# Attention with an exponential on two engines: two of VectorE's four shifted forms summed by an accumulating transfer, with six shared homes

## The chip, the cores and the metric

The kernel runs on one core of a Trainium2 chip. The metric is the device time of one execution in microseconds (us). Before the change it is 793.76 us, the median of three runs (793.5 to 793.86). The core's engines that matter here are TensorE (PE, matrix products), ScalarE (ACT, exponentials and tanh), VectorE (DVE, elementwise work), GpSimd (POOL) and the queues that issue transfers (SP's above all). They run side by side, each through its own instructions in program order, and wait for each other by semaphores.

## The reference

Two blocks read the same x (2048 rows of 512, bfloat16) and are mixed row by row by a gate:

```python
qkv = (x @ wqkv) in 32 heads of 16            # x: 2048 x 512, wqkv: 512 x 1536
p = softmax(q @ k.T * 16 ** -0.5)             # per head, 2048 x 2048
a = (p @ v) @ wo                              # attention
b = (silu(x @ w_gate) * (x @ w_up)) @ w_down  # 512 -> 1792 -> 512
g = sigmoid((x * gate_w).sum(-1))
out = g * a + (1 - g) * b
```

The costly part is the softmax: 32 heads x 2048 x 2048 exponentials, some 134 million.

## The kernel before

**Units and tiles.** Queries are cut into 4 blocks of 512 (`QB`), heads into 8 groups of 4 (`G`); a block and a group make one of 32 units. A unit has 16 tiles of 128 keys (`KT`); a tile is 4 heads x 128 keys x 512 queries. The scores of a tile come as two pairs of heads; the product with the values adds up in one PSUM bank for the whole unit (`o_ps`), which VectorE copies out at the unit's end (`post`, called from `close`). The values have a column of ones beside each head's 16, so that the softmax's denominator comes out of the same product.

**Two ways to the exponential.** For most tiles ACT takes it from a pair's scores, 128 x 1024 at a time (`emit_pair`, tiles `s_t` to `e_t`), and PE multiplies the result with the values in one group of four column matmuls (`pv`). For the others PE writes the scores of one head after another into `d_t`, often beside a pair's score matmuls in rows of the array that those leave free, and VectorE computes (`emit_d`, `first`) a 16-bit integer `y_t` = EXP_A x score + EXP_B, whose bits, read as bfloat16, are a coarse power of two. It then makes four copies of the whole tile, (y + shift) x 0.25 with four shifts (`copy`, tiles `c_t`), and PE multiplies each of the four with the values: the sum of the four forms is the smoother exponential. Such a tile thus costs VectorE four times 128 x 512 from PSUM and four times 128 x 2048 in SBUF, and PE four groups of column matmuls where a tile of ACT's costs one.

**Homes.** A copy lies in one of `NS` = 4 homes, taken in turn: three buffers of the pool `vex`, and one that is the first head group's keys (`kaug[:, 0]`) once these are used up, or four rows of `wd_t` before. The profile therefore shows copies under three names, `c_t`, `kaug` and `wd_t`. A home comes free when the product of its copy has run. ACT's results have `EB` = 10 buffers.

**The order of the work.** The order of every engine's instructions is written out when the program is built, by a planner (`Plan`) that keeps a clock for each engine: 0.216 us for a group of column matmuls and for a pair of scores, 0.1 for a change between row and column use of the array, 0.906 for an exponential (`ACT_US`), 0.6 for a VectorE instruction. In the main loop it emits the next pair of scores when the bank it needs comes free, and fills PE's time before that with products (`emit_pv`) and with pieces of other work (`side`, `put_piece`): projections, the feed-forward block's `gu` and `ops` chains, gate logits. These pieces wait in chains with a release and a due slot (`Pacer`). `fill_dve` gives VectorE its work by the plan's clock. `v_unit` says whether a further tile may go to VectorE: its work must end 8 us (`LEAD`) before the unit's exponentials do. `want_d` says how many `d_t` may be emitted now, from the three spare PSUM banks (`banks`), less one if a column chain is next. `hi[un]` is the number of ACT's tiles in a unit. If `EB - 1` pairs wait for their product, a product is forced (`next_pv`).

**The gate.** `gate_pieces` multiplies x with `gate_w` in eight visits of eight matmuls with one column each (`glog`), and clips each result on VectorE into `ge`; `gate_end` takes the exponential. `gate_w` is loaded by `late_loads`, called at slot 28 in program order; SP's queue runs ahead of that, as nothing there waits. The values of heads 4 to 31 come from `v_pieces`, 16 chains of four groups (`vp`, 448 columns each).

All matmuls go through one helper line (L160), all ACT instructions through L163, VectorE's and SP's through L172, so groups are told apart by tile names.

Of the kernel before, what the change touches and what calls it, by code (L numbers as in the profile page):

```python
# [9 lines left out]
ALU = mybir.AluOpType  # L10
AX = mybir.AxisListType
BF16 = mybir.dt.bfloat16
F32 = mybir.dt.float32
U16 = mybir.dt.uint16
# [65 lines left out]
def kernel(  # L80
# [32 lines left out]
    SLOTS = UNITS * KT  # L113

    UNIT = [(qb, 0) for qb in range(QB)] + [(qb, g) for qb in range(QB) for g in range(1, G)]
    EB = 10
    NY = 3
    NV = 4
    NC = 4
    NS = 4  # L120

# [49 lines left out]

    vec = Ordered(nc.vector)
    queue = Ordered(nc.sync)


    xT = big.tile([P, DC, S], BF16, name="xT")
# [24 lines left out]
    wo_l = big.tile([P, 2, D], BF16, name="wo_l")  # L203

    def late_loads():
        queue.dma_start(out=gw_col[:], in_=gate_w.rearrange("(dc p) -> p dc", p=P))
        queue.dma_start(out=wo_t[:], in_=A_wo.rearrange("(b p) d -> p b d", p=P))
        for i in range(2):
            for j in range(4):
                h = H - 8 + 4 * i + j  # L210
                queue.dma_start(out=wo_l[32 * j + 1:32 * j + 1 + DH, i, :], in_=A_wo[h * DH:(h + 1) * DH, :])
# [92 lines left out]
    def spend(mode, mms, ready=0.0):  # L304

        plan.seq += 1
        work_at.append((plan.pe, mms))
        plan.pe = max(plan.pe + (0.1 if mode != plan.mode else 0.0), ready) + (0.226 if mode == "F" else 0.216) * mms
        plan.mode = mode

    def later(cost, f, ready=None, key=None):

        c = plan.chain
        if c is not None:
            c.owed += 1
        ready = plan.pe + 0.25 if ready is None else ready
        owed.insert(sum(o[0] <= ready for o in owed), (ready, cost, f, c, key))
# [41 lines left out]
    def m_free(ps, t):  # L359
        i = [h is ps for h in held].index(True)  # L360
        banks[i], held[i] = t + 0.2, None
# [137 lines left out]
    def v_pieces(tt):  # L499

        def end(p):
            dst = vaug[:, tt, 4 * VC:G * 4 * VC].rearrange("p (h c) -> p h c", c=VC)[:, :, 1:1 + DH]
            vec.tensor_copy(out=dst, in_=p[:, 64:D].rearrange("p (h c) -> p h c", c=DH))
            m_free(p, plan.dve)
        return columns(DC, "vp", lambda dc: xT[:, dc, tt * P:(tt + 1) * P], lambda dc: wv[:, dc, 64:D],
                       lambda p: later(0.54, lambda: end(p)), c0=64)

# [103 lines left out]
        return [(1, f, True)]  # L613


    def gate_pieces(t0):
        def f():
            gp = m_tile("glog")
            for t in (t0, t0 + 1):
                for dc in range(DC):  # L620
                    mm(gp[:, t:t + 1], lhsT=xT[:, dc, t * P:(t + 1) * P],
                       rhs=gw_col[:, dc:dc + 1], start=(dc == 0), stop=(dc == DC - 1))
            spend("F", 2)

            def end():
                vec.tensor_scalar(out=ge[:, t0:t0 + 2], in0=gp[:, t0:t0 + 2], scalar1=-40.0, scalar2=40.0,
                                  op0=ALU.max, op1=ALU.min)
                m_free(gp, plan.dve)
            later(0.15, end)
        return [(0.7, f, True, "F", None)]  # L630

    def gate_end():
        act(out=ge[:, :], in_=ge[:, :], func=ACT.Exp, scale=-1.0)
        plan.act += 0.2
# [73 lines left out]
    e_of = {}  # L708
    at = {}
    vops = []  # L710
    c_turn = [0]
    c_free = [0.0] * NS
    pv_turn = [True]
    vready = []
# [85 lines left out]
    waiting = {}  # L800
    copies = {}

    def copy(n, k, y):
        i = c_turn[0] % NS
        c_turn[0] += 1
        if i < NS - 1:
            c = vex.tile([P, NV * QBW], U16, tag="c", name="c_t", bufs=NS - 1)[:, :]
        else:
            c = (kaug[:, 0, :] if au > QB else wd_t[:, 0:4, :].rearrange("p f d -> p (f d)")).bitcast(U16)
        plan.dve = max(plan.dve, c_free[i])  # L810
        c_free[i] = 1e9
        vec.tensor_scalar(out=c, in0=y[:, :], scalar1=SHIFTS[k], scalar2=0.25, op0=ALU.add, op1=ALU.mult)
        copies[n, k] = (c.bitcast(BF16), i)
        vready.append((plan.dve + 0.3, n, k))
        if k == NC - 1:
            y_live[0] -= 1

    def c_ready():
        return c_free[c_turn[0] % NS]

    def pay_d():
        ready, f, _ = d_wait.pop(0)
# [49 lines left out]
        part_done.append(0)  # L872

    def pv_left(un):
        return hi[un] - done_a[un] + NC * (KT - hi[un]) - done_v[un]

    def pv(n, k=None):

        un = n // KT
        if un not in o_of:  # L880
            while un and un - 1 not in osbs:
                pay()
            plan.pe = max(plan.pe, o_end[0])
            o_of[un] = ps_o.tile([P, QBW], F32, tag="o", name="o_ps")
        if v_of(n) is not None:
            force(v_of(n))
        o = o_of[un]
        first = pvs[un] in ((0, KT // 2) if un == 0 else (0,))
        last = un == 0 and pvs[un] == KT // 2 - 1 or pv_left(un) == 1
        if k is not None:  # L890
            c, slot = copies.pop((n, k))
        for i, b in enumerate(range(4 * n, 4 * n + 4)):
            j = HEADS[i]
            c0 = (4 * UNIT[un][1] + j) * VC
            mm(o[32 * j:32 * j + 32, :], lhsT=vaug[:, n % KT, c0:c0 + 32],
               rhs=e_of.pop(b) if k is None else c[:, i * QBW:(i + 1) * QBW],
               start=first, stop=last, tile_position=(0, 32 * j), skip_group_check=True)
            e_left.pop(b, None)
        pvs[un] += 1
        if un == 0 and pvs[0] == KT // 2:  # L900
            later(0.6, take_part, plan.pe + 0.47)
        spend("C", 1, 0.0 if k is not None else max(e_end.pop(b, 0.0) for b in range(4 * n, 4 * n + 4)))
        if k is None:
            done_a[un] += 1
        else:
            done_v[un] += 1
            c_free[slot] = plan.pe + 0.2
# [197 lines left out]
    pace = Pacer()  # L1105
    need = {}
    q_of = {}

    def k0_pieces(tb):

# [43 lines left out]
    need[9] = [v_late]  # L1154
    need[14] = [parts]
    q_of[0] = again
    v_rest = [pace.add(v_pieces(tt), 2, int(12 + 3 * tt)) for tt in range(KT)]

    def v_of(n):

# [12 lines left out]
    for qb in range(QB):  # L1173
        for b in range(NB):
            d = UNIT.index((qb, max(2 * b, 1))) * KT
            after = []
            if qb == 0:
                ks = []
                for tb in range(QB):
                    prev = [pace.add(k_pieces(b, tb), 0, d - 40 + tb, prev)]  # L1180
                    ks += prev

                def bnd(b=b):
                    later(2.46, lambda: k_bound(b))
                after = prev = [pace.add([(0.2, bnd, False)], 0, d - 34, ks)]

            if b == 0:
                rel = UNIT.index((qb - 1, 2)) * KT + 1 if qb else 0
            elif b == 1:
                rel = UNIT.index((qb - 1, 6)) * KT + 1 if qb else 0  # L1190
            else:
                rel = UNIT.index((qb, 2 * b - 2)) * KT + 1 if (qb, b) != (0, 2) else UNIT.index((0, 2)) * KT + 1
            q = pace.add(q_pieces(qb, b), rel, d - 25)
            bc = pace.add(bound_pieces(qb, b), rel, d - 22, [q] + after, 2)
            need.setdefault(d - 12, []).append(bc)
            for g in {max(2 * b, 1), 2 * b + 1}:
                q_of[UNIT.index((qb, g))] = bc
    gates = [pace.add(gate_pieces(2 * i), 36 + 7 * i, 44 + 7 * i) for i in range(KT // 2)]
    gates = [pace.add([(0.2, gate_end, False)], 40, 106, gates)]
    turned = pace.add([(1, turn_odds, True, "F", None)], 40, 130, gates, 2)  # L1200
    need.setdefault(160, []).append(turned)

# [118 lines left out]
    def begin(n):  # L1321
        plan.slot = n
        for c in need.get(n, []):
            force(c)
        if n == 28:
            late_loads()
        i = n - (QB + 1) * KT - 8
        if 0 <= i < 2 * FC and i % 4 == 0:
            wd_load(i // 2)
        for f in at.pop(n, []):  # L1330
            f()
        pace.begin_slot(n)
# [89 lines left out]
    def want_d():  # L1422
        if not vcur and v_unit() is None:
            return 0
        c = pick()
        one = c is not None and c.pieces[c.i][2] and (pace.credit > 0 or c.deadline <= plan.slot + 4)
        open_ = sum(b is not None and b <= plan.pe for b in banks)
        return max(0, min(2, open_ - int(one), 3 - len(d_wait)))

    while au < UNITS:  # L1430
# [10 lines left out]
        if room > 0.02:  # L1441
# [4 lines left out]
            col = c is not None and (c.pieces[c.i][3:] or "C")[0] == "C"  # L1446
            urgent = c is not None and c.deadline < 0 and back < EB - 4
            visit = len(n_pv) + (len(c.pieces) - c.i if col else 0)
            if n_pv and fits > 0 and not urgent and (plan.mode == "C" or visit > 1 and fits > 1 and (pv_turn[0] or c is None or col)
                                      or back >= EB - 4 or (c is None or col) and fits == 1):  # L1450
                emit_pv(n_pv[0])
                pv_turn[0] = False
                continue
# [113 lines left out]
```

## Time and profile before

| | |
|---|---|
| median of 3 runs | 793.76 us (793.5 to 793.86) |
| the profiled execution | 792.79 us, span 791.1 us |
| PE, ACT, DVE busy | 766.0, 776.4, 723.0 us |
| POOL busy | 11.0 us, all in the first 20 us |
| exponentials on ACT | 806, that is 403 of 512 tiles |
| copies on VectorE (`c_t`, `kaug`, `wd_t`) | 327 + 96 + 13 = 436, that is 109 tiles |
| granted TensorE clock | 0.999 |
| DMA engines | 17.4% busy, 32.73 MB in 88145 packets |

A line of the groups reads: line, engine, operation, written tile <- read tiles, shapes, count | busy time, mean ns of one | idle time before and what ended it. Matmuls and exponentials are pipelined: the next starts before the last has ended, so a mean of 384 ns or 1101 ns is longer than the distance between two starts. A line of the waits reads: who <- waited for whom: us in total, times, longest. A line of the timeline reads: start, duration of the merged run, engine, line, operation, tiles, count.

### The profile page before, as it was taken

Reading aid. Unit: us, or ns where it says so; the run is one execution under the profiler, and the core shown is the slowest. Engines: PE = TensorE matmul, PEld = TensorE weight load, DVE = VectorE, ACT = ScalarE, POOL = GpSimd, SP = SyncE. Lnnn points to the kernel's source line nnn. Section 1 sums busy time; section 2 is a strip of 40 time slices with the busy share of each in tenths; the row PEclk is TensorE's granted clock in tenths of the full one; section 3 lists DMA queues with packets and bytes.
Section 4 is the critical chain, followed back from the end, with each engine's and each line's share of the span. In section 5 each row is a group of like instructions: output and inputs, shape, how many; then the busy total and the mean of one; then the engine's idle time right before and its main releaser. Section 6 shows DMA issues by size and latency. Waiting matters only on the chain.

```text
span 791.1 us, 22892 instructions
## 1 busy us (share of the span) xinstructions
PE 766.0 (97%) x9445; PEld 225.5 (29%) x9445; DVE 723.0 (91%) x1224; ACT 776.4 (98%) x875; POOL 11.0 (1%) x34
## 2 busy tenths in 40 slices
PE   8999999999999999999999999999999999999997
PEld 3322232322222222232222222222222222222222
DVE  7799998889799999999999899999999998899993
ACT  6999999999999999999999999999999999999996
POOL 5000000000000000000000000000000000000000
PEclk9999999999999999999999999999999999999999
DMA  9000103243200012220100032111000222100001
GB/s 215 7 2 17 30 9 60 64 111 84 64 19 8 13 37 64 49 58 17 40 15 19 10 99 54 45 35 33 14 18 14 58 66 63 41 12 13 17 25 35
DMA packets 88145, 32.73 MB, mean 41 GB/s; under 512 B 74304, under 2 KB 87592, under 8 KB 88040
## 3 DMA queue, kind: packets, MB, share of 16 engines
q1 hardware_dynamic: 86312, 30.93, 16.4%
q8 instruction: 74, 1.21, 0.7%
q10 hardware_dynamic: 1728, 0.33, 0.2%
q14 instruction: 31, 0.25, 0.1%
HBM read 21.55 MB, written 2.35 MB: 30 GB/s over the span
## 4 chain that ended last, share of the span: by engine, by line
PE 49%; ACT 40%; issue 9%; DVE 1%; DMA 1%; ACTq 0%; DVEq 0%
ACT e_t L163 37%; PE s_t L160 17%; PE o_ps L160 15%; PE gu L160 8%; PE ops L160 5%; ACT th L163 2%; PE qp L160 1%; PE kp L160 1%; PE dps L160 1%; DMA wd_t<-in_A_x_dram 1%; PE vp L160 0%; PE bp L160 0%; DVE y_t L172 0%; DVE mt L172 0%; DVE c_t L172 0%
## 5 line engine op out<-in xcount | busy, mean ns | idle before, releaser
L163 ACT ACTIVATE e_t<-s_t 128x1024 bf16<-128x1024 f32 x806 | 752.6, 1101 | 1.6 <-PE s_t L160 1.1
L172 DVE TENSOR_SCALAR y_t<-d_t 128x512 uint16<-128x512 f32 x436 | 291.5, 686 | 33.6 <-PE d_t L160 31.1
L160 PE MATMUL s_t<-qx,kaug 32*128 32x512 bf16 (+1 forms) x1276 | 248.4, 384 | 13.6 <-ACT e_t L163 11.2
L172 DVE TENSOR_SCALAR c_t<-y_t 128x2048 uint16<-128x2048 uint16 x327 | 216.8, 687 | 0.4
L160 PEld LDWEIGHTS <-kaug 32*128 32x128 bf16 (+1 forms) x2048 | 88.4, 91 | 337.3 <-issue 332.9
L160 PE MATMUL o_ps<-e_t,vaug 128*32 128x512 bf16 x1612 | 158.9, 387 | 0.0
L160 PE MATMUL o_ps<-c_t,vaug 128*32 128x512 bf16 x1308 | 125.5, 386 | 0.0
L160 PE MATMUL d_t<-qx,kaug 32*128 32x512 bf16 x356 | 123.9, 384 | 0.0
L160 PEld LDWEIGHTS <-vaug 128*32 128x32 bf16 x3368 | 72.1, 94 | 122.9 <-issue 116.5
L160 PE MATMUL gu<-xT,wg 128*32 128x512 bf16 x896 | 78.6, 382 | 0.0
L160 PE MATMUL gu<-xT,wu 128*32 128x512 bf16 x896 | 74.9, 381 | 0.0
L172 DVE TENSOR_SCALAR kaug<-y_t 128x2048 uint16<-128x2048 uint16 x96 | 65.8, 686 | 0.0
L160 PE MATMUL ops<-wd_t,mt 128*32 128x512 bf16 x672 | 59.1, 382 | 0.0
L172 DVE SCALAR_TENSOR_TENSOR gs<-th,gu 128x512 bf16<-128x512 bf16 x56 | 38.3, 683 | 4.7 <-ACT th L163 4.5
L172 DVE SCALAR_TENSOR_TENSOR mt<-gs,gu 128x512 bf16<-128x512 bf16 x56 | 38.3, 683 | 2.5 <-PE gu L160 1.0
L160 PE MATMUL s_t<-q,kaug 32*128 32x512 bf16 (+1 forms) x200 | 38.9, 385 | 0.9 <-ACT e_t L163 0.5
L160 PE MATMUL o_ps<-kaug,vaug 128*32 128x512 bf16 x384 | 37.9, 384 | 0.0
L163 ACT ACTIVATE th<-gu 128x512 bf16<-128x512 f32 x56 | 37.9, 676 | 0.0
L160 PEld LDWEIGHTS <-mt 128*32 128x32 bf16 (+1 forms) x1037 | 25.9, 95 | 29.1 <-issue 21.2
L160 PEld LDWEIGHTS <-wu 128*32 128x32 bf16 x896 | 22.1, 96 | 18.4 <-issue 8.3
L160 PEld LDWEIGHTS <-wg 128*32 128x32 bf16 x896 | 20.5, 95 | 19.2 <-issue 13.6
L160 PE MATMUL vp<-rb,xT 128*32 128x448 bf16 (+1 forms) x320 | 21.8, 323 | 0.0
(138 smaller groups left out, 372.4 us busy)
## 6 DMA issues: line engine op xcount, KB each, us to landing
wg<-in_B_w_gate_dram SPq DMA_DIRECT2D x56, 128.0 KB
wu<-in_B_w_up_dram SPq DMA_DIRECT2D x56, 128.0 KB
on<-osb SPq DMA_DIRECT2D x120, 16.0 KB
rb<-rr SPq DMA_DIRECT2D x15, 128.0 KB
wd_t<-in_B_w_down_dram SPq DMA_DIRECT2D x7, 256.0 KB
qx<-qst SPq DMA_DIRECT2D x96, 16.0 KB
out_dram<-o_t SPq DMA_DIRECT2D x12, 128.0 KB
kaug<-on SPq DMA_DIRECT2D x20, 64.0 KB
```

What stands on the lines that cost most here:

```text
L160: return ordered(nc.tensor.matmul(*args, **kw))
L163: ordered(nc.scalar.activation(*args, **kw))
L172: return lambda *a, **kw: ordered(f(*a, **kw))
```

## The change

Five things are done.

1. For a tile of VectorE's, the first two of the four copies may be summed by a transfer that POOL issues (`pool.dma_start(..., accum_op=ALU.add)`), from the first copy's home into the second's. PE then multiplies three results for this tile, not four (`merged` keeps count for `pv_left`). It is done where, by the plan, the unit ends more than 0.6 + 5.5 + 1.0 us later and more than one home (`SPARE`) is free; the sum is taken as ready 5.5 + 0.3 us after the second copy.
2. There are six homes: four of `vex`, the one of before, and half of the projection weights `wqk` once the keys are projected. The one that comes free first by the plan is taken. `EB` goes from 10 to 8.
3. The gate's logits become one more column of the values' product: column 63 of `wv`, free once the first heads' values are made, receives `gate_w`, and VectorE clips that column of each result. `gate_pieces` goes.
4. The planner counts 0.223 us for a group of column matmuls.
5. `want_d` leaves no bank for a column chain while fewer than two copies wait, and a short column chain that has begun goes ahead of products.

```diff
-    EB = 10
+    EB = 8
-    NS = 4
+    NS = 6
+    SPARE = 1
+    pool = Ordered(nc.gpsimd)
     def late_loads():
-        queue.dma_start(out=gw_col[:], in_=gate_w.rearrange("(dc p) -> p dc", p=P))
-        plan.pe = max(...) + (0.226 if mode == "F" else 0.216) * mms
+        plan.pe = max(...) + (0.226 if mode == "F" else 0.223) * mms
...
             vec.tensor_copy(out=dst, in_=p[:, 64:D].rearrange("p (h c) -> p h c", c=DH))
+            vec.tensor_scalar(out=ge[:, tt:tt + 1], in0=p[:, 63:64], scalar1=-40.0, scalar2=40.0, op0=ALU.max, op1=ALU.min)
...
-        return columns(DC, "vp", ..., lambda dc: wv[:, dc, 64:D], lambda p: later(0.54, lambda: end(p)), c0=64)
+        return columns(DC, "vp", ..., lambda dc: wv[:, dc, 63:D], lambda p: later(0.69, lambda: end(p)), c0=63)
-    def gate_pieces(t0):
...
+    first_of = {}
+    merged = [0] * UNITS
+    ADD_US = 5.5
+    homes = [(lambda i=i: vex.tile([P, NV * QBW], U16, tag=f"c{i}", name="c_t")[:, :].rearrange("p (i q) -> p i q", q=QBW),
+              lambda: True) for i in range(NS - 2)]
+    homes += [(lambda: (kaug[:, 0, :].rearrange("p (i q) -> p i q", q=QBW) if au > QB else wd_t[:, 0:4, :]).bitcast(U16),
+               lambda: True),
+              (lambda: wqk[:, :, D:2 * D].bitcast(U16), lambda: keys_done[-1].done())]
+
+    def unit_end(un):
+        return plan.act + ((hi[un] - (at_ if un == au else 0)) * TILE_US if un >= au else 0.0) + (
+            (hi[au] - at_) * TILE_US if un > au else 0.0)
+
+    def c_slot():
+        return min((i for i in range(NS) if homes[i][1]()), key=lambda i: c_free[i])
     def copy(n, k, y):
-        i = c_turn[0] % NS
-        c_turn[0] += 1
...
+        i = c_slot()
         plan.dve = max(plan.dve, c_free[i])
         c_free[i] = 1e9
-        vec.tensor_scalar(out=c, in0=y[:, :], scalar1=SHIFTS[k], scalar2=0.25, op0=ALU.add, op1=ALU.mult)
-        copies[n, k] = (c.bitcast(BF16), i)
-        vready.append((plan.dve + 0.3, n, k))
+        c = homes[i][0]()
+        vec.tensor_scalar(out=c, in0=y[:, :].rearrange("p (i q) -> p i q", q=QBW), scalar1=SHIFTS[k], scalar2=0.25,
+                          op0=ALU.add, op1=ALU.mult)
+        c = c.bitcast(BF16)
+        copies[n, k] = (c, i)
+        if k == 0 and unit_end(n // KT) - plan.dve > 0.6 + ADD_US + 1.0 and sum(
+                h[1]() and f <= plan.dve + 0.6 for h, f in zip(homes, c_free)) > SPARE:
+            merged[n // KT] += 1
+            first_of[n] = copies.pop((n, k))
+        elif k == 1 and n in first_of:
+            c0, slot = first_of.pop(n)
+            pool.dma_start(out=c, in_=c0, accum_op=ALU.add)
+            c_free[slot] = plan.dve + ADD_US
+            vready.append((plan.dve + ADD_US + 0.3, n, k))
+        else:
+            vready.append((plan.dve + 0.3, n, k))
...
-        return hi[un] - done_a[un] + NC * (KT - hi[un]) - done_v[un]
+        return hi[un] - done_a[un] + NC * (KT - hi[un]) - merged[un] - done_v[un]
...
-    v_rest = [pace.add(v_pieces(tt), 2, int(12 + 3 * tt)) for tt in range(KT)]
+    def gate_column():
+        later(0.1, lambda: vec.tensor_copy(out=wv[:, :, 63:64], in_=gw_col[:].unsqueeze(2)))
+    gate_w_in = pace.add([(0.2, gate_column, False)], 9, 11, [v_late])
+    v_rest = [pace.add(v_pieces(tt), 2, int(14 + 3 * tt), [gate_w_in]) for tt in range(KT)]
...
-    gates = [pace.add(gate_pieces(2 * i), 36 + 7 * i, 44 + 7 * i) for i in range(KT // 2)]
-    gates = [pace.add([(0.2, gate_end, False)], 40, 106, gates)]
+    gates = [pace.add([(0.2, gate_end, False)], 40, 106, v_rest)]
...
+        if n == 3:
+            queue.dma_start(out=gw_col[:], in_=gate_w.rearrange("(dc p) -> p dc", p=P))
...
         open_ = sum(b is not None and b <= plan.pe for b in banks)
+        if len(vops) < 2:
+            one = False
...
+            going = col and 0 < c.i and len(c.pieces) < 6 and back < EB - 3
-            if n_pv and fits > 0 and not urgent and (plan.mode == "C" or ...
+            if n_pv and fits > 0 and not urgent and not going and (plan.mode == "C" or ...
```

More of the change, by code (lines that the diff above doesn't have):

```diff
@@ L307, in spend @@
         work_at.append((plan.pe, mms))
-        plan.pe = max(plan.pe + (0.1 if mode != plan.mode else 0.0), ready) + (0.226 if mode == "F" else 0.216) * mms
+        plan.pe = max(plan.pe + (0.1 if mode != plan.mode else 0.0), ready) + (0.226 if mode == "F" else 0.223) * mms
         plan.mode = mode
@@ L503, in end @@
             vec.tensor_copy(out=dst, in_=p[:, 64:D].rearrange("p (h c) -> p h c", c=DH))
+            vec.tensor_scalar(out=ge[:, tt:tt + 1], in0=p[:, 63:64], scalar1=-40.0, scalar2=40.0, op0=ALU.max, op1=ALU.min)
             m_free(p, plan.dve)
-        return columns(DC, "vp", lambda dc: xT[:, dc, tt * P:(tt + 1) * P], lambda dc: wv[:, dc, 64:D],
-                       lambda p: later(0.54, lambda: end(p)), c0=64)
+        return columns(DC, "vp", lambda dc: xT[:, dc, tt * P:(tt + 1) * P], lambda dc: wv[:, dc, 63:D],
+                       lambda p: later(0.69, lambda: end(p)), c0=63)
     qx = [big.tile([P, 2, 2, QBW], BF16, name=f"qx{i}") for i in range(2)]
@@ L613, in bound_pieces @@
         return [(1, f, True)]
-    def gate_pieces(t0):
[L617 to L630, printed above, removed]
     def gate_end():
@@ L710 @@
     vops = []
-    c_turn = [0]
     c_free = [0.0] * NS
@@ L801 @@
     copies = {}
-    def copy(n, k, y):
-        i = c_turn[0] % NS
-        c_turn[0] += 1
[L806 to L809, printed above, removed]
+    first_of = {}
[3 more added lines that the diff above has]
+              lambda: True) for i in range(NS - 2)]
@@ L810, in copy, with c_ready @@
+    def c_ready():
+        return c_free[c_slot()]
+    def copy(n, k, y):
+        i = c_slot()
         plan.dve = max(plan.dve, c_free[i])
         c_free[i] = 1e9
-        vec.tensor_scalar(out=c, in0=y[:, :], scalar1=SHIFTS[k], scalar2=0.25, op0=ALU.add, op1=ALU.mult)
-        copies[n, k] = (c.bitcast(BF16), i)
-        vready.append((plan.dve + 0.3, n, k))
+        c = homes[i][0]()
[14 more added lines that the diff above has]
+            vready.append((plan.dve + 0.3, n, k))
@@ L815, in copy @@
         if k == NC - 1:
             y_live[0] -= 1
-    def c_ready():
-        return c_free[c_turn[0] % NS]
     def pay_d():
@@ L895, in pv @@
             mm(o[32 * j:32 * j + 32, :], lhsT=vaug[:, n % KT, c0:c0 + 32],
-               rhs=e_of.pop(b) if k is None else c[:, i * QBW:(i + 1) * QBW],
+               rhs=e_of.pop(b) if k is None else c[:, i, :],
                start=first, stop=last, tile_position=(0, 32 * j), skip_group_check=True)
@@ L1107 @@
     q_of = {}
+    keys_done = []
     def k0_pieces(tb):
@@ L1181 @@
                     ks += prev
+                    keys_done.append(prev[0])
                 def bnd(b=b):
@@ L1448 @@
             visit = len(n_pv) + (len(c.pieces) - c.i if col else 0)
-            if n_pv and fits > 0 and not urgent and (plan.mode == "C" or visit > 1 and fits > 1 and (pv_turn[0] or c is None or col)
+            going = col and 0 < c.i and len(c.pieces) < 6 and back < EB - 3
+            if n_pv and fits > 0 and not urgent and not going and (plan.mode == "C" or visit > 1 and fits > 1 and (pv_turn[0] or c is None or col)
                                       or back >= EB - 4 or (c is None or col) and fits == 1):
```

## The prediction

> **What bounds the kernel now.** I read the page's busy shares first: which engine could set the end at all.
>
> ```profile
> PE 766.0 (97%) x9445; PEld 225.5 (29%) x9445; DVE 723.0 (91%) x1224; ACT 776.4 (98%) x875; POOL 11.0 (1%) x34
> ACT e_t L163 37%; PE s_t L160 17%; PE o_ps L160 15%; PE gu L160 8%; PE ops L160 5%; ACT th L163 2%; PE qp L160 1%; PE kp L160 1%; PE dps L160 1%; DMA wd_t<-in_A_x_dram 1%; PE vp L160 0%; PE bp L160 0%; DVE y_t L172 0%; DVE mt L172 0%; DVE c_t L172 0%
> ```
>
> Two engines are full and the chain changes between them; VectorE hardly appears in it, and POOL is free. Next the groups and the waits:
>
> ```profile
> L163 ACT ACTIVATE e_t<-s_t 128x1024 bf16<-128x1024 f32 x806 | 752.6, 1101 | 1.6 <-PE s_t L160 1.1
> L172 DVE TENSOR_SCALAR y_t<-d_t 128x512 uint16<-128x512 f32 x436 | 291.5, 686 | 33.6 <-PE d_t L160 31.1
> L172 DVE TENSOR_SCALAR c_t<-y_t 128x2048 uint16<-128x2048 uint16 x327 | 216.8, 687 | 0.4
> L160 PE MATMUL o_ps<-c_t,vaug 128*32 128x512 bf16 x1308 | 125.5, 386 | 0.0
> L160 PE MATMUL glog<-gw_col,xT 128*128 128x1 bf16 x64 | 2.7, 165 | 0.0
> ...
> DVE y_t L172 <- PE d_t L160: 31.1, 58, 1.7
> PE s_t L160 <- ACT e_t L163: 12.8, 41, 1.0
> PEld L160 <- DMA wu<-in_B_w_up_dram: 0.7, 3, 0.2
> ```
>
> Exponentials overlap, so small waits of ACT vanish in "busy". The timeline shows them: a run of six that is undisturbed, and one that is not.
>
> ```profile
> 307.40 5.63 ACT L163 ACTIVATE e_t<-s_t 128x1024 bf16<-128x1024 f32 x6
> 297.06 5.71 ACT L163 ACTIVATE e_t<-s_t 128x1024 bf16<-128x1024 f32 x6
> ```
>
> (5.63 - 1.10) / 5 is 0.906 us from start to start, (5.71 - 1.10) / 5 is 0.922. Over all 806 the shortest distance is 0.903, the mean 0.922: 14.9 us of hidden waits in all. 1.4 us of them lie before 40 us. Distances up to 20 ns over the floor make 2.9 us, and a step of about 65 ns comes back every 3.7 us whatever PE does, near 4 us in all. What is left for a less busy PE to give back is some 6.5 us.
>
> PE by starts: from 40 to 770 us a group of four column matmuls follows another after 0.2165 us (1015 times), a change from scores to columns takes 0.322 (752), and back 0.322 at the shortest (751). That is 220 + 242 + 242 = 704 us of 730. ACT's floor in its exponentials' stretch (12.8 to 783.0) is 806 x 0.9035 + 56 x 0.477 (one tanh) = 755 of 770. So PE is full, but ACT is the last bound: PE's relief alone is worth 6.5 us; the rest must come by moving tiles to VectorE. A tile moved takes two exponentials, 1.81 us, from ACT and gives VectorE eight instructions of 0.604 (start to start), 4.8 us.
>
> **The change, part by part.**
>
> Merged forms. 436 copies are 109 tiles. I followed each copy to its product by order. The first copies of 94 tiles end over 7.1 us before the last exponential of their unit, which is what the new test asks for; some fail for want of a home. A merged tile holds two homes for some 6.5 us and two for about 1.5, 16 home-us of the 6 x 7 that pass per tile, so homes rarely forbid it. I take 90 merges, 60 to 100 as ends. Each removes one group of four o_ps matmuls: 90 x 0.2165 = 19.5 us of PE. PE's 704 us hide all of it but ACT's 6.5.
>
> The transfer itself: 90 x 512 KB from SBUF to SBUF, adding. No row shows an adding transfer, nor one issued by POOL. The nearest row is the plain SBUF copy for the keys:
>
> ```profile
> 59.98 2.53 SPq L172 DMA_DIRECT2D kaug<-on  x4
> kaug<-on SPq DMA_DIRECT2D x20, 64.0 KB
> ```
>
> Its first packet starts 1.3 us after the issue began. Its 4096-byte packets take 0.23 to 0.58 us, median 0.36; a merge puts eight on each of 16 engines, so 2.9 us, 4.2 with the start. That is the lower end. The upper end doubles the data time, as the sum has to be read too: 1.3 + 5.8 = 7.1. The planner counts 5.5 and lets PE use the sum 0.3 later. I take 5.5 or a little less, since the plain copy is the nearest row, and charge 0.7 us for a few late ones. The chain's first piece, 512 KB from HBM in 4.80 us, lies between the ends. The Trainium skill, "DMA: Bandwidth & Descriptors", section "Anatomy of one DMA", gives about 2.0 us fixed plus bytes / 436 GB/s for a POOL transfer. An estimate from that page is 3.2 us, below all of this, for a plain copy; it would make no transfer late.
>
> DMA engines: 90 x 8 x 0.36 = 261 us each, 33% of the span on top of 17%. Weight loads wait longer in their engines, but they are asked for two chunks ahead and PE waits 0.7 us for them now. Cost nothing; if that cover were gone, three waits of 0.2 would become some hundred of about 0.5.
>
> The new wait: POOL's issue waits for VectorE's second copy and for whatever last used the home. Behind it on POOL stand only further merges (POOL's 11 us lie at the start); PE waits for the sum, and behind PE's product stand the scores for ACT. That wait is the one that could hurt.
>
> VectorE beside POOL. No row shows POOL at work beside the copies. Ends: nothing, and one copy's 0.604 us per merge, 54 us. At 723 of 791 it has 68 us idle, 43.6 of them between 40 and 770 us. I take nothing, as the trace has no row in which one engine of the two waits for the other's port. The copies' new shape (4 runs of 512) I take at the old 0.687: casts in 28 runs of 16 (vaug<-vp, 0.625) cost no more than flat ones of their size. The skill's page "SBUF — State Buffer", "Who interferes with whom", speaks against this change: VectorE's fast two-port forms of tensor_scalar and POOL's descriptor writing exclude each other for a whole instruction. By that rule a copy issued just after the second one holds the descriptors back by 0.6 us, and a copy that finds POOL at work waits in turn; the sum would then use the 54 us end, where the forecast uses none.
>
> More tiles on VectorE. VectorE's largest wait is 31.1 us for d_t, 58 times. With fewer than two copies outstanding, d_t no longer leaves a bank for a column chain, and PE has room. All 31.1 would be 31.1 / 4.8 = 6 tiles; in the stretches from 200 to 700 us it is busy 94 to 96%, so it cannot be had in full. I take three: 3 x 1.81 = 5.4 us off ACT. VectorE then has 723 + 14.5 + 1.2 = 739 of 780, 94.7%, like those stretches. Ends: none, and five (9 us).
>
> Gate logits. Eight visits of eight glog matmuls go: one stands between scores at 90.90 and 91.64, 0.74 apart where a bare pair needs about 0.32, so 0.42 x 8 = 3.4 us of PE, hidden like the rest. One more column in 448 of the v products is nothing. VectorE's clips become 16 of 0.150 instead of 8: 1.2 us in its idle time. The gate is now complete only after the last v chain, due at slot 59, well before its own due slot of 106.
>
> Moved load. gw_col is issued at 12.50 us and nothing waits before it on SP; wo_t follows in both kernels. Nothing.
>
> EB 10 to 8. At each pair's start I counted the pairs whose products were still to come: 2 or 3 nearly always, 6 once. The new limit is 7. Nothing, unless late sums hold a unit's end.
>
> The planner's 0.223 for a group (0.2165 column to column, 0.322 with a change against its 0.323) puts PE where it really is; that is how the 6.5 us are found. The rule that keeps a begun column chain together saves a change of 0.1 here and there; taken as nothing.
>
> Sum on the profiled execution (792.79, span 791.1 and 1.69 around it): -6.5 - 5.4 + 0.7 = -11.2, 781.6. The median shown is 0.97 higher: 782.6.
>
> **Rivals.**
>
> (1) Late sums, slower. A sum that takes L us from the second copy reaches PE L - 5.8 late. ACT stands one pair ahead, which covers some 0.35. At 7.1 us the rest is 0.95 x 90 = 86 us of PE waiting against 23 freed and 26 idle: +37, less the gain's 11: about 820. Break-even is near 6.6 (0.45 x 90 = 41 us, most of it covered). For it: the upper end above; against: the plain copy's 4.2.
>
> (2) VectorE is held by POOL. With 54 us more it would be busy 777 of 780 and set the end; its idle time cannot be used that well, so at its present 95% the span is 818 at that end, and at half, 27 us, about 790 to 795. For it: copies fill a third of VectorE's time. Against: POOL needs the port only for descriptors.
>
> (3) Hidden anyway. PE's work was never the last bound, d_t is held up by banks, no tile moves: 793.8 - 6.5 = 787, or nearer 791 if the small waits stay.
>
> (4) Few merges. If plan time at unit ends or homes forbid most of them, 30 remain: 6.5 us of PE, half the waits: 789.
>
> **How the numbers follow.** Forecast 0.50, with its own range 775 to 787 (no tile or five, waits wholly or half recovered). Rivals 3 and 4 together 0.17, of which 0.05 within 0.2%. Rival 1 0.20, rival 2 0.13. Within 0.2% (1.6 us) is about what a measurement can tell from no change. Faster 0.50 + 0.12 = 0.62, same 0.05, slower 0.33. 80% from 771 (more tiles than five) to 814, which cuts off the far ends of rivals 1 and 2.
>
> **What would show it.** Right: o_ps<-c_t and its like fall by some 360 matmuls (90 groups); e_t falls from 806 to about 800 while y_t rises to 448; y_t's wait for d_t falls below 20 us; PE's wait for e_t rises, as ACT is now the bound; waits of PE for a sum stay under 10 us. Wrong: PE or its weight loads waiting tens of us for a DMA into c (rival 1); c_t's mean over 687 ns or VectorE idle before c_t with no releaser (rival 2); e_t still 806 (rival 3); under 40 transfers on POOL's queue (rival 4). The weakest step is the transfer's time, which no row of this profile has.

## The result and the profile after

The changed kernel takes 816.66 us (median of six runs, 813.94 to 819.33) against 793.81 for the kernel before in the same measurement: a ratio of 1.0288, interval 1.0278 to 1.0299. It is slower by 22.9 us; I had forecast 782.6. The profiled execution of the changed kernel has a span of 813.9 us, 22.8 more than before.

The page's busy shares, four of its groups, POOL's queue and three of its transfers' rows (size in KB, median us from issue to landing):

```profile
PE 760.9 (93%) x9137; PEld 223.1 (27%) x9137; DVE 741.1 (91%) x1265; ACT 771.6 (95%) x867; POOL 102.6 (13%) x109
...
L164 ACT ACTIVATE e_t<-s_t 128x1024 bf16<-128x1024 f32 x798 | 749.6, 1115 | 26.1 <-PE s_t L161 18.1
L173 DVE TENSOR_SCALAR y_t<-d_t 128x512 uint16<-128x512 f32 x452 | 300.0, 683 | 25.5 <-PE d_t L161 22.9
L173 DVE TENSOR_SCALAR c_t<-y_t 128x2048 uint16<-128x2048 uint16 x315 | 210.7, 688 | 1.2 <-PE o_ps L161 1.2
L161 PE MATMUL o_ps<-c_t,vaug 128*32 128x512 bf16 x1080 | 102.3, 386 | 17.5 <-DMA c_t<-c_t 11.8
...
q0 software_dynamic: 20784, 39.33, 28.7%
...
c_t<-c_t POOLq DMA_DIRECT2D x26, 512.0 KB, 5.3
c_t<-wqk POOLq DMA_DIRECT2D x13, 512.0 KB, 5.9
wqk<-c_t POOLq DMA_DIRECT2D x11, 512.0 KB, 6.0
```

Much of what the change sets out to do is there. 75 tiles are merged. VectorE has taken 452 / 4 = 113 tiles, four more than before, and ACT eight exponentials fewer. VectorE's copies last 688 ns in the mean, 687 before. But ACT now idles 26.1 us before its exponentials, where it idled 1.6, and PE waits before its products. The waits name what for:

```profile
PE o_ps L161 <- DMA c_t<-c_t: 11.8, 7, 6.1
PE o_ps L161 <- DMA wqk<-c_t: 5.9, 8, 1.4
PE o_ps L161 <- DMA c_t<-wqk: 3.0, 5, 1.1
PE o_ps L161 <- DMA c_t<-kaug: 2.0, 3, 1.4
PE o_ps L161 <- DMA kaug<-c_t: 1.3, 2, 1.0
PE o_ps L161 <- DMA kaug<-wqk: 1.3, 1, 1.3
```

25.3 us in 26 waits, all for a sum that has not landed. The distances from one exponential's start to the next give the account. What they have over the floor of 0.903 us (called ACT's waits below) makes 41.7 us, where it made 14.9: +26.8. Eight exponentials fewer: -7.2. The first exponential comes 0.9 us later, and the end comes 2.3 us later behind the last one. Together +22.8, the whole difference.

The longest wait, in the timeline:

```profile
683.19 0.61 PE L161 MATMUL d_t<-qx,kaug 32*128 32x512 bf16 x2
683.35 1.94 ACT L164 ACTIVATE e_t<-s_t 128x1024 bf16<-128x1024 f32 x2 [0.23 <-PE s_t L161]
683.97 1.28 DVE L173 TENSOR_SCALAR y_t<-d_t 128x512 uint16<-128x512 f32 x2
684.60 1.34 POOL L173 DMA_DIRECT2D c_t<-c_t  x1 [17.57 <-DVE c_t L173]
685.17 0.68 DVE L173 TENSOR_SCALAR c_t<-y_t 128x2048 uint16<-128x2048 uint16 x1
...
689.91 0.62 PE L161 MATMUL o_ps<-c_t,vaug 128*32 128x512 bf16 x4 [6.11 <-DMA c_t<-c_t]
690.29 1.09 PE L161 MATMUL o_ps<-e_t,vaug 128*32 128x512 bf16 x8
691.14 1.09 PE L161 MATMUL gu<-xT,wu 128*32 128x512 bf16 x8
```

The reader should compare two times: PE stands at the product from 683.8, and POOL issues the transfer only at 684.60. A planned time that is too short does not explain that; the planner had forced the product there, ready or not (below). ACT and VectorE run dry behind it. Two results of ACT's are ready and are multiplied at once afterwards (x8 at 690.29), so a ready product stood behind one that was not.

How late the sums are: from the end of the second copy to landing it takes 4.9 to 8.8 us, in the median 6.22, and 51 of 75 take longer than the 5.8 that the plan allows before PE may use them. (The expectations below have 47 of 75, and medians of 6.5 and 5.65 by homes; counted from each tile's own second copy these are 51, 6.6 and 5.8.) The trace gives the parts. A flat transfer (between homes that lie in one piece in each partition) that nothing disturbs: 0.54 from the copy's end to POOL's start, 0.86 of POOL's work, 0.57 to the first packet, eight packets of 0.339 in each DMA engine, and about 0.3 to landing, 5.0 in all. Three things add to it. With over 100 KB of SP's traffic beside it, POOL's end to landing is 4.84 in the median against 3.79 with under 10 KB (19 and 10 flat transfers). A transfer into or out of the strided home `wqk`, which lies in runs of 512 elements and moves in packets of 1024 bytes, lands 6.60 us after the copy in the median, a flat one 5.81. And VectorE's copies hold POOL back:

```profile
451.27 2.20 POOL L173 DMA_DIRECT2D c_t<-c_t  x1 [10.01 <-DVE c_t L173]
```

```profile
450.90 1.27 DVE L173 TENSOR_SCALAR y_t<-d_t 128x512 uint16<-128x512 f32 x2
452.10 0.67 DVE L173 TENSOR_SCALAR kaug<-y_t 128x2048 uint16<-128x2048 uint16 x1
452.70 0.68 DVE L173 TENSOR_SCALAR wqk<-y_t 128x2048 uint16<-128x2048 uint16 x1
453.30 0.67 DVE L173 TENSOR_SCALAR y_t<-d_t 128x512 uint16<-128x512 f32 x1
```

POOL's work ends at 453.47, 0.09 after the second of the two copies, where it would have been done at 452.13. A copy that starts 0.5 to 0.63 us after POOL makes POOL's 0.86 us some 1.3 in case after case; one that ends within 0.68 us of POOL's start, and instructions from PSUM (`y_t`) beside it, leave it at 0.85 to 0.88 in nearly all cases. By the rule of the Trainium skill's "SBUF — State Buffer", "Who interferes with whom", the two exclude each other for a whole instruction, whichever came first. The trace agrees on POOL's side, for copies that start late in its work. On VectorE's side it shows no such block: the 96 copies that run beside POOL's work last 702 ns in the mean, the others 683, 1.8 us in all.

### The profile page after: what moved, and what is told of

Same layout as the page of the kernel before. It is cut to its first block, busy times and chain, and to the rows that moved or that the text cites. A ratio compares the mean times of both kernels' runs of the same rounds, so it can differ in the third digit from the quotient of the medians.

```text
span 813.9 us, 22502 instructions
## 1 busy us (share of the span) xinstructions
PE 760.9 (93%) x9137; PEld 223.1 (27%) x9137; DVE 741.1 (91%) x1265; ACT 771.6 (95%) x867; POOL 102.6 (13%) x109
## 3 DMA queue, kind: packets, MB, share of 16 engines
q1 hardware_dynamic: 86312, 30.93, 16.2%
## 5 line engine op out<-in xcount | busy, mean ns | idle before, releaser
L164 ACT ACTIVATE e_t<-s_t 128x1024 bf16<-128x1024 f32 x798 | 749.6, 1115 | 26.1 <-PE s_t L161 18.1
L173 DVE TENSOR_SCALAR y_t<-d_t 128x512 uint16<-128x512 f32 x452 | 300.0, 683 | 25.5 <-PE d_t L161 22.9
L173 DVE TENSOR_SCALAR c_t<-y_t 128x2048 uint16<-128x2048 uint16 x315 | 210.7, 688 | 1.2 <-PE o_ps L161 1.2
L161 PE MATMUL o_ps<-c_t,vaug 128*32 128x512 bf16 x1080 | 102.3, 386 | 17.5 <-DMA c_t<-c_t 11.8
L161 PE MATMUL gu<-xT,wu 128*32 128x512 bf16 x896 | 68.5, 385 | 0.0
L173 POOL DMA_DIRECT2D c_t<-c_t x26 | 29.8, 1146 | 227.9 <-PE d_t L161 78.0
L173 DVE TENSOR_SCALAR kaug<-y_t 128x2048 uint16<-128x2048 uint16 x70 | 48.0, 685 | 0.0
L173 DVE TENSOR_SCALAR wqk<-y_t 128x2048 uint16<-128x2048 uint16 x59 | 40.4, 684 | 0.0
L161 PE MATMUL s_t<-q,kaug 64*128 64x512 bf16 (+1 forms) x192 | 37.4, 384 | 1.3 <-ACT e_t L164 1.0
L161 PEld LDWEIGHTS <-mt 128*32 128x32 bf16 (+1 forms) x1037 | 25.1, 95 | 29.0 <-issue 22.9
L173 POOL DMA_DIRECT2D wqk<-c_t x11 | 16.6, 1510 | 108.9 <-DVE wqk L173 24.6
L173 POOL DMA_DIRECT2D c_t<-wqk x13 | 18.7, 1440 | 85.0 <-PE d_t L161 35.7
```

The source lines that it names most:

```text
L161: return ordered(nc.tensor.matmul(*args, **kw))
L164: ordered(nc.scalar.activation(*args, **kw))
L173: return lambda *a, **kw: ordered(f(*a, **kw))
```

## The experiments

All times are medians in us; ratios are against the kernel before on the same chip, with their 95% intervals. Theory A: sums that land later than the plan has them hold PE, and ACT starves. Theory B: the other edits cost the time. Theory C: the transfers do, whoever waits for them.

**All of the change but the sums.**

```diff
-        if k == 0 and unit_end(n // KT) - plan.dve > ...
+        if False and unit_end(n // KT) - plan.dve > ...
```

> All of the change but the sums: no transfer is issued, PE takes four products for every tile. Theory A (the sums arrive later than the plan has them, PE waits, ACT starves): the 24 us of PE's waits for a DMA are gone and ACT's waits fall from 41.7 us back to about 15; with the few more tiles on VectorE that the other edits give, 785 to 794 us. Theory B (the other edits cost the time: eight buffers for ACT's results, the planner's 0.223, the order of column chains): it stays at 805 us or more, though no sum is late.

794.25, ratio 1.0008 (0.9999 to 1.0018). B falls: without sums the change costs nothing. ACT's waits are 14.0 us. A gain of the other edits is there, 804 exponentials and 110 tiles on VectorE, and is given back in the tail, the time behind the last exponential (11.9 us for 8.0): the last exponential ends at 780.7 (783.0 before), and then the timeline shows work that used to be done by then:

```profile
779.53 2.55 PE L161 MATMUL ops<-wd_t,mt 128*32 128x512 bf16 x44
784.40 0.62 PE L161 MATMUL o_ps<-e_t,vaug 128*32 128x512 bf16 x8
```

**A later sum in the plan.**

```diff
-    ADD_US = 5.5
+    ADD_US = 7.5
```

> ADD_US 7.5 in place of 5.5: the plan takes a sum as ready 7.8 us after the second copy; in the changed kernel 47 of 75 sums landed later than the 5.8 us planned there, but only 2 later than 7.8. Theory A: PE's waits for a DMA fall under 4 us, fewer tiles are merged (the test asks for 9.1 us before the unit's end), and the time is 780 to 792 us. Theory C (it is the transfers themselves, beside VectorE or other transfers, whenever they are used): with most of the merges left it stays at 803 us or more.

803.24, ratio 1.0116 (1.0097 to 1.0136), with 68 merges. A miss for A as I had stated it, and by its bare number C's case. Its trace shows two stalls and no more: 4.5 us for a sum at 481.9 and 3.5 us for a weight load at 647.5, with 26.7 us of ACT's waits in all. The small waits that A is about are gone; what is left is of another kind, a weight load and a forced product:

```profile
PE o_ps L161 <- DMA c_t<-c_t: 4.5, 1, 4.5
PE gu L161 <- DMA wg<-in_B_w_gate_dram: 3.5, 1, 3.5
```

**Forced products by readiness.**

```diff
-        emit_pv(pv_list(None)[0])
+        when = {v[1:]: v[0] for v in vready}
+        emit_pv(min(pv_list(None), key=lambda t: when[t] if len(t) > 1 else max(e_end[b] for b in ...)))
```

> Where a product is forced (the buffers for ACT's results nearly full) the one that is ready first by the plan is taken, not the first of VectorE's list. The longest wait of the changed kernel, 6.1 us at 689.9, and perhaps the 2.6 us at 66.8, are of this kind: PE reached the product 0.8 us before POOL even issued the transfer. Theory A with forced products as a part of it: 804 to 810 us, those long waits gone, the many waits of 0.2 to 1.4 us left. If forced products carry most of it: below 798. If they carry nothing: 814 to 819.

804.92, ratio 1.0147 (1.0120 to 1.0175), as expected. The wait at 689.9 is gone. The one at 66.8 is not (2.15 us at 66.6), so it was a late sum and no forced product (in the changed kernel, of a transfer that took 8.8 us). `next_pv` had taken the head of VectorE's list, ready or not, whenever the buffers of ACT's results ran full. Before the change that was harmless, as the plan has a copy ready 0.3 us after it is made.

**Transfers that nobody waits for.**

```diff
-    NS = 6
+    NS = 5
+            pool.dma_start(out=aside[...], in_=c, accum_op=ALU.add)   # after the second copy
+            hold[i] = plan.dve + ADD_US + 1.5                         # its home is held as long
-            pool.dma_start(out=c, in_=c0, accum_op=ALU.add)
```

> Four products for every tile, and a transfer all the same: POOL adds the second copy into a buffer that nobody reads, at the same places in the order, with the homes held as long. It has the transfers' cost without any wait for a sum. Theory A: as the kernel without sums, 785 to 794 us, within 4 us of it. Theory C (POOL's descriptors against VectorE's copies, or traffic): 800 us or more, with VectorE's copies longer than 690 ns in the mean or idle time before them.

798.82, ratio 1.0064 (1.0049 to 1.0079): 4.6 us above the kernel without sums, between the two theories' numbers, with 85 transfers, more than the changed kernel has. It has five homes, as the buffer that nobody reads takes the place of one; that this costs nothing was not tried by itself, but 804 exponentials and 110 tiles on VectorE are the same as without sums. VectorE's copies last 685 ns in the mean, with 0.5 us of idle time before them, so VectorE is hardly held. It is the loads that share the DMA engines:

```profile
308.93 1.45 SPq L173 DMA_DIRECT2D wg<-in_B_w_gate_dram  x1
...
311.28 0.61 PE L161 MATMUL gu<-xT,wg 128*32 128x512 bf16 x8 [1.59 <-DMA wg<-in_B_w_gate_dram]
```

In the kernel without sums, whose time runs 0.5 us ahead here, this load is issued at 304.72. In this kernel a transfer comes before it, from 301.61 to its landing at 308.08, with only 7 packets of SP's queue between 305 and 306. PE waits 1.6 and 1.5 us for weights, at 311.3 and 545.7, and ACT loses 1.9 and 1.7 at these two places, 3.6 of the 4.6. C is thus a part, through the weights, and a small one.

**Both mends of lateness.** ADD_US 7.5 and forced products by readiness.

> Both mends of lateness at once: ADD_US 7.5, and a forced product is the one that is ready first. With 7.5 alone two stalls were left, 4.5 us for a forced sum and 3.5 us for a weight load from HBM. Theory A: the first goes, the second stays in some place, 795 to 800 us, PE's waits for a DMA into a copy under 2 us. If it stays above 802 the forced product is not what it was taken for.

793.22, ratio 1.0003 (0.9989 to 1.0016). All 23 us are back, with 64 merges and their transfers still made. The profiled execution, the fastest of the ten (791.65, span 789.9), has 0.3 us of waits for a sum, and 15.1 us of ACT's waits, as before the change:

```profile
PE o_ps L161 <- DMA c_t<-c_t: 0.3, 1, 0.3
```

That settles A: forced and late sums were the loss. It is no gain either, which asks what the relief of PE is worth:

**The ideal sum.** For merged tiles the first form is neither moved nor multiplied, and the second is ready at once.

```diff
-            pool.dma_start(out=c, in_=c0, accum_op=ALU.add)
-            vready.append((plan.dve + ADD_US + 0.3, n, k))
+            vready.append((plan.dve + 0.3, n, k))
```

> The ideal sum: no transfer and no delay. For the tiles that the changed kernel merges, the first of the four forms is left out of the result (a part of the computation, its product with the values, is left out), so PE takes three products, all ready at once; the copy itself is still made and its home held. It gives what relief of PE alone is worth. My prediction's step (6.5 us of ACT's waits and three tiles): 781 to 786 us. Rival 3 of the prediction (PE's work was hidden, ACT and VectorE set the end): within 3 us of the kernel without sums, 791 to 797.

789.74, ratio 0.9959 (0.9944 to 0.9973), above my 781 to 786 and outside rival 3's 791 to 797. So a sum without any delay is worth some 4 us against the kernel without sums (1.0008; the two were measured beside the kernel before on different chips, so I compare ratios). Its groups beside those of the kernel before:

```profile
L164 ACT ACTIVATE e_t<-s_t 128x1024 bf16<-128x1024 f32 x800 | 749.0, 1143 | 3.9 <-PE s_t L161 2.2 <-PE d_t L161 1.3
L173 DVE TENSOR_SCALAR y_t<-d_t 128x512 uint16<-128x512 f32 x448 | 296.5, 681 | 18.0 <-PE d_t L161 16.6
```

Two more tiles have gone to VectorE than without sums (112 for 110; four exponentials, 3.6 us). ACT's waits have not shrunk: 16.2 us with 79 groups of products fewer on PE than without sums, where they were 14.0. The rest of the gain is in the tail, 9.3 us for 11.9. What I had taken for PE's lateness in them is not cured by a lighter PE.

**Flat homes.** Five homes, without `wqk`.

```diff
-    NS = 6
+    NS = 5
-              (lambda: wqk[:, :, D:2 * D].bitcast(U16), lambda: keys_done[-1].done())]
```

> Five homes, without the strided one in wqk. In the changed kernel the sums that touch wqk land 6.5 us after the second copy in the median (26 of them, 1024-byte packets), the others 5.65 (49). Theory A: fewer and smaller waits, but the flat ones' tail and the forced products remain: 803 to 811 us. If the strided home carries the lateness alone: below 798. If it carries nothing: 814 to 819.

803.10, ratio 1.0117 (1.0085 to 1.0148): at the fast end of its range, with 68 merges. The median from copy to landing is 5.63 here, POOL's part 0.86. The strided home is a part of the lateness.

**Due times, and the two together.** Three kernels ask whether the tail and the sums can both be had: the kernel without sums with the feed-forward block due 12 slots earlier; flat homes, ADD_US 6.5 and products by readiness; and these with a due time 6 slots earlier. A fourth gives the six homes with ADD_US 7.5 that due time.

```diff
-    f0, f1 = 72, SLOTS - 8
+    f0, f1 = 72, SLOTS - 20        # SLOTS - 14 where it says so
```

> The kernel without sums, with the feed-forward block due 12 slots earlier (SLOTS - 20 for SLOTS - 8). Without sums the last exponential ended 2.3 us earlier than before the change, but the last products of values 1.5 us later, behind 2.5 us of ops products in the tail. If that is what eats the gain: 788 to 792 us. If the earlier due time crowds the earlier slots instead: 793 us or more.

793.25, ratio 1.0003 (0.9994 to 1.0013). The tail is 8.0 us again, but the exponentials are 806 again and VectorE's tiles 109: the earlier due time takes back what the tail cost.

> Flat homes only, ADD_US 6.5 (a sum ready 6.8 us after the second copy; in the flat kernel nine in ten land within 7.05, half within 5.6), forced products by readiness. More tiles can be merged than with 7.5. Theory A: under 3 us of waits for a DMA into a copy, 790 to 796 us; no better than the 789.7 us of the ideal sum, since that is all that PE's relief is worth.

796.97, ratio 1.0037 (1.0027 to 1.0048), a little above its range. Waits for a sum are 0.4 us; a weight load costs PE 2.2 at one place (640.6), and the tail is 11.2.

> The same with the feed-forward block due 6 slots earlier (SLOTS - 14). With 12 slots earlier and no sums the tail behind the last exponential went from 11.9 to 8.0 us, but two more tiles' worth of exponentials came back to ACT. If half the shift keeps the tail short and the tiles on VectorE: 787 to 792 us, faster than both kernels. If the tail was a matter of the sums' waits: the same as without the shift.

790.96, ratio 0.9963 (0.9948 to 0.9977): faster than both kernels. No wait for a sum is left in its waits, and 0.2 us before a matmul for a weight of the feed-forward block:

```profile
PE gu L161 <- DMA wg<-in_B_w_gate_dram: 0.2, 1, 0.2
```

> Six homes with the strided one, ADD_US 7.5, forced products by readiness, and the due time of SLOTS - 14. The profile without the shift had 10.0 us behind the last exponential, 2 more than before the change. If the shift takes these two: 789 to 792 us against 793.2. If not: 793 or more.

794.91, ratio 1.0020 (1.0006 to 1.0035): no help here. Its profile has three waits for a weight load (5.0 us, the longest 2.8), its tail is 9.4.

**Control, and weights earlier.** The faster kernel without its sums; and with them, the weights loaded three chunks ahead (and seven buffers for ACT's results, which makes the room).

```diff
-    ffnw = ctx.enter_context(tc.tile_pool(name="ffnw", bufs=3))
+    ffnw = ctx.enter_context(tc.tile_pool(name="ffnw", bufs=4))
-                w_load(i + 2, True)
+                w_load(i + 3, True)
-    EB = 8
+    EB = 7
```

> The control for the kernel of 791.0 us: the same five flat homes and the same due time, without sums. If the sums carry its gain: 793 to 795 us. If the due time carries it alone: 789 to 791.5.

792.78, ratio 0.9992 (0.9983 to 1.0001). Flat homes and due time alone give nothing clear; of the 2.8 us that the faster kernel is under the kernel before, some 2.3 are its sums' (0.9963 against 0.9992).

> The kernel of 791.0 us with the weights of the feed-forward block loaded three chunks ahead, not two, for which ACT's results have seven buffers, not eight. If the rare stalls of 1 to 3 us for a weight load are what makes the runs with sums scatter (788.9 to 793.1): the longest runs go, 788 to 791 us, and no wait for wg or wu is over 0.5 us. If seven buffers force products: slower, 793 or more.

789.88 (789.38 to 790.51), ratio 0.9957 (0.9944 to 0.9969). The scatter has shrunk from 4.2 to 1.1 us, though over fewer runs. The longest wait for a weight is 0.2, and seven buffers cost nothing that the time shows. It is level with the ideal sum, and not clearly faster than the kernel of 0.9963, whose one profile had no long wait for a weight either; that earlier weights help is thus not shown. Whether they would without sums was not tried.

```profile
L164 ACT ACTIVATE e_t<-s_t 128x1024 bf16<-128x1024 f32 x802 | 751.0, 1145 | 2.8 <-PE s_t L161 2.3 <-PE d_t L161 0.3
PE o_ps L161 <- DMA c_t<-c_t: 0.4, 1, 0.4
PEld L161 <- DMA wu<-in_B_w_up_dram: 0.2, 1, 0.2
```

## Why the prediction was wrong

**The step that failed: the transfer's time and what lateness costs.** I wrote "I take 5.5 or a little less, since the plain copy is the nearest row, and charge 0.7 us for a few late ones". The range of 4.2 to 7.1 held the median of 6.22. The choice within it was too low, but not for the data's part: adding packets take 0.339 us, no more than the plain copy's 0.363, so the doubling that made my upper end does not happen. What I had left out is the 0.54 from copy to POOL, POOL's 0.86 to 1.5, the hold by VectorE's copies, and SP's traffic. The charge was wrong by far more: 25.3 us of PE's waits and 26.8 of ACT's for 0.7.

**Rival 1 was the right mechanism with a wrong break-even.** I had it turn at 6.6 us, on the sum that 0.45 x 90 is "most of it covered" by PE's freed and idle time. The median was under that and the kernel lost 22.9. A wait is not paid out of PE's total idle time; it falls at one place, and what is not covered there by ACT's one pair is lost. The spread counts, not the median: a sum of 8.8 us costs 2.6 in one place, and one of 4.9 gives nothing back. The forced product, 6.1 us in one wait, I had not seen at all, though I named a unit's end under EB as a place where late sums could matter.

**The gain.** "Three tiles" was right: four came, and 798 exponentials against the 800 of my sum. "6.5 us of ACT's waits" was wrong: with the ideal sum they stay at 16.2. So the change with an ideal sum was worth 3.5 us (789.74 against 793.22), not 11, and the forecast would have been too low by 7 even with every sum in time.

**Weight loads.** "Cost nothing" held in the changed kernel, whose waits have none for `wg` or `wu`. It failed in five of the other kernels with transfers: not a hundred waits of 0.5, but one to three, the longest 0.9 to 3.5 us, near bursts of SP's own loads.

**Merges.** 75 for 90: within the ends, of no weight. **VectorE beside POOL** (rival 2): VectorE's copies lose 1.8 us in all to it, not 27 or 54; what the copies do is hold POOL back, and so it belongs to rival 1. **Gate, moved load, buffers**: the kernel without sums, at 794.25, shows that these together cost nothing; singly they were not tried. Of EB it holds only without sums: a full set of buffers is what forces a product.

## What to carry to other kernels

In an order that is written out ahead, a transfer's planned time must cover its spread, not its median: each late one stops an in-order engine on the spot, and early ones earn nothing. Every place that picks work "because something must be picked" has to know which of it is ready, once one kind of work can be late by microseconds. And the worth of relieving an engine can be measured before the relief is built, by leaving that work out: here it was some 4 us, and the kernels that came up to it with real transfers had a longer planned time, products by readiness, flat homes and an earlier due time.

## What the runs showed of the hardware that was not expected

The granted clock halves after a stretch in which PE was only partly busy, and a long wait is not needed for it. The windows around the 6.1 us wait (microseconds, busy time with counts of PE, PEld, DVE, ACT and POOL, then the granted clock, DMA share and GB/s):

```profile
679.00:680.00 1.00, 0.43 (x7) 0.16 (x4) 1.00 (x3) 1.00 (x2) 0.00 (x0) 1.00 0.00 0
680.00:681.00 1.00, 0.58 (x8) 0.20 (x7) 1.00 (x3) 1.00 (x2) 0.00 (x0) 1.00 0.00 0
681.00:682.00 1.00, 0.54 (x6) 0.28 (x3) 1.00 (x3) 1.00 (x2) 0.00 (x0) 1.00 0.03 8
682.00:683.00 1.00, 0.69 (x6) 0.20 (x5) 1.00 (x3) 1.00 (x2) 0.00 (x0) 0.79 0.00 0
683.00:684.00 1.00, 0.80 (x6) 0.21 (x5) 1.00 (x3) 0.78 (x2) 0.00 (x0) 0.50 0.01 4
684.00:686.00 2.00, 0.00 (x0) 0.00 (x0) 1.85 (x4) 1.29 (x2) 1.34 (x1) 0.50 0.09 26
686.00:690.00 4.00, 0.09 (x4) 0.09 (x7) 0.00 (x0) 0.00 (x0) 0.00 (x0) 0.50 0.88 167
690.00:692.00 2.00, 2.00 (x20) 0.60 (x19) 0.00 (x0) 0.00 (x0) 0.00 (x0) 0.50 0.00 0
692.00:694.00 2.00, 2.00 (x24) 0.46 (x20) 0.59 (x1) 1.12 (x2) 0.00 (x0) 0.80 0.00 0
694.00:696.00 2.00, 2.00 (x30) 0.53 (x25) 1.89 (x4) 2.00 (x3) 0.00 (x0) 1.00 0.29 66
```

PE waits from 683.8, but the clock is at half from 682.6, after a stretch from 679 to 682 in which PE was busy for 0.43 to 0.58 of each microsecond. The kernel with products by readiness has no long wait there, and its clock falls all the same (0.53 from 683 to 684) and is full again by 687. In the changed kernel it stays at 0.50 until 692.8, through the wait and for nearly 3 us of full work behind it; pairs of column groups take 1.09 us where they take 0.61 (690.29 and 694.47 in the timeline). ACT loses 7.7 us at this place to PE's 6.1. Behind the wait of 2.6 us at 66.8 the clock is still full until 68.2, then 0.54 from 68 to 70 us and 0.60 from 70 to 72, and ACT loses 4.2 us there, 1.3 of them in that half clock; behind the one of 1.4 us at 481.1 it stays at 1.00. The Trainium skill's "TensorE: Matmul & The Clock Gate", Part 1, gives some 3.4 us of busy time until the clock is full again; here it is full 2.9 us after the long wait, and the half clock at 68.2 lasts 3.4 us.

An adding transfer moves its 4096-byte packets in 0.339 us in the median, no slower than the plain copy's 0.363.
